# Five pieces of work in other places of a hand-ordered gated-mix backward kernel, steps 3 to 7

## The chip, the cores and the metric

The kernel runs on one core of a Trainium2 chip. A core has five engines, each with its own in-order instruction queue: TensorE (PE, matmuls; its weight loads are listed as PEld), VectorE (DVE), ScalarE (ACT), GpSimd (POOL) and SyncE (SP, which here only starts DMAs). They wait for each other on semaphores. SBUF is the working memory, PSUM takes the results of matmuls. The metric is the device time of one execution in microseconds (us).

## The reference

Forward, and then the gradients of all inputs but one, for 2048 tokens of width 576 in bf16:

```
g   = sigmoid((x * gate_w).sum(-1))                    # one gate a token
a   = irfft2(rfft2(x) * (w_r + 1j * w_i))              # spectral branch on A_x
b   = (gelu(x @ w_gate) * (x @ w_up)) @ w_down         # feed-forward branch, width 4608
out = g * a + (1 - g) * b
```

The outputs are `out` and the gradients with respect to x, w_r, w_i (2048 x 289), w_gate, w_up (576 x 4608), w_down (4608 x 576) and gate_w, given `grad_out` (dO). The feed-forward branch needs, for each feature, the gate and up products of x, the product z of dO with w_down, and from these the arrays A (gelu times up), dHg and dHu, which go into the weight gradients and, in the second stage, into `out` and the gradient of x.

## The kernel before

**Two stages.** Stage one takes the 4608 features in 18 groups of 256 (loop `g`, L992) and, within a group, the 16 token tiles of 128 in four steps of four tiles (loop `m`, L996). The step number is `pr = 4 g + m`, so steps 0 to 3 are group 0, steps 4 to 7 group 1. Stage two multiplies A, dHg and dHu, read back from DRAM, with the weights. The order of every engine's work is the order in which the Python code emits it: there is no scheduler.

**One step.** `H_mm` (L403) issues 16 + 4 matmuls for z (L413, L418) and the first four for gate|up (L422). `H_da` (L438) copies z out of PSUM on ACT, scaled by 1 - g (L441). Then `xy_full(0)` and `xy_full(1)` (L424) issue eight gate|up matmuls each (L429), a half each: two token tiles in one PSUM tile `xy`, of which there are two. With a second argument, `xy_full` calls that function between the two tiles of its half. `H_act` (L444) takes a half out of PSUM on ACT: part 1 copies gate to `xb` and up to `hu` (L450, L451), part 0 squares gate into `q` (L448). `H_ew1` (L453) computes the argument `s` of a sigmoid on DVE (L456 to L460).

**The held sigmoid.** `sigs` calls `H_ew2` (L471): a sigmoid on ACT (L476), eight DVE operations after it for groups 0 and 1 (L487 to L497), which give A, dHu and dHg, and a store of these that is put on a list and issued by SP at a later `flush`. In steps 0 to 3 `sigs` is put into `held` and called in the next step, between the halves of gate|up. From step 4 on it is called at the end of its own step, so that step 4 calls it twice: for step 3 and for itself.

**The rest of a step** is the weight gradient of the group before (`W_units`, L520), four matmuls at a time or eight: `u_dwd` for w_down (L541, with dO in `dB` as the streamed side), `u_dw` for gate|up (L559) and a tail (L573). Each unit has one of two PSUM tiles `wps` and ends with a copy `wevac` (L510) on ACT, or on DVE while `wcopy[0]` is `VC` (step 6). Step 4 issues the first 12 of 16 token tiles of two `u_dw` units, step 5 their last four and two `u_dwd`, step 6 the tail, two `u_dwd` and half a `u_dw`. Since `dB` must be scaled by 1 - g before `u_dwd` uses it, `scale_dB(k, ...)` (L985) scales token tiles 4k to 4k + 3, on ACT (L988) or DVE (L990).

**Spectral pieces** are small units (a list `fft`, L933) that `fft_next` emits one by one; `want` (L957) says how many a step has: one in step 6, four in step 7. In these steps they are by turns `u1` (L602: six matmuls, then an ACT copy Y, L607) and `u2` (L619: two matmuls, an ACT copy `ve`, L622, two DVE operations L624 and L625, a store). All use the one PSUM tile `z`, as does z of the steps. `k0` is 1 where the first piece of a step goes into `xy_full(1)`; before, that is so from step 8 on.

**Tables.** `build_R` (L157) makes integer angles on DVE in step 5; `build_B` (L215) is a generator, started in step 1 and resumed by `next(makeB)` twice in step 6: first nine DVE operations (L232 to L238), and at the end of the step one product (L248). Between them `run_late` (L114) emits five sines on ACT (L177, L245), with a table load before them and one before the next sigmoid.

Buffers that matter: `xb`, `hu` and `da` have two each; `q` and `s` one each from group 1 on, so that a new `q` waits until DVE has read the old one in L493.

Of the kernel before, what the change touches and what calls it, by code (L numbers as in the profile page):

```python
# [113 lines left out]
def run_late(tb):  # L114
    while tb.late:
        tb.late.pop(0)()
# [139 lines left out]
def kernel(  # L256
# [176 lines left out]
    def ewt(tag, g):  # L433
        if tag in ("q", "s", "sg"):
            return unit([4, FG], name=tag) if g == 0 else ew.tile([P, 4, FG], BF16, tag=tag, name=tag, bufs=1)
        return ew.tile([P, 4, FG], BF16, tag=tag, name=tag, bufs=2)

    def H_da(g, m, z):  # L438
        da = ewt("da", g)
        for t in range(4):  # L440
            nc.scalar.activation(da[:, t, :], z[:, t % 2, t // 2, :], ACT.Copy, scale=omg32[:, 4 * m + t:4 * m + t + 1])  # L441
        return da

    def H_act(k, xy, tiles, part):  # L444
        xb, q, hu = tiles
        h = slice(2 * k, 2 * k + 2)
        if part == 0:
            nc.scalar.activation(q[:, h, :], xy[:, :, 0:FG], ACT.Square)  # L448
        else:
            nc.scalar.copy(xb[:, h, :], xy[:, :, 0:FG])  # L450
            nc.scalar.copy(hu[:, h, :], xy[:, :, FG:2 * FG])  # L451
# [13 lines left out]
    def flush(n=9):  # L465

        while stores and n:
            stores.pop(0)()
            n -= 1
# [422 lines left out]
    VC, AC = V.tensor_copy, nc.scalar.copy  # L892
# [23 lines left out]
    makeB = build_B(nc, tb, unit, res)  # L916
# [20 lines left out]
    def fft_next():  # L937
        while fft_pos[0] < len(fft):
            u = fft[fft_pos[0]]
            fft_pos[0] += 1  # L940
            u()
            if not getattr(u, "noslot", False):
                return

    def ready():
        u = fft[fft_pos[0]]
        return not hasattr(u, "needs") or u.needs()
# [4 lines left out]
    NPR = NT // 2  # L952
# [4 lines left out]
    def want(pr):  # L957

        n0 = FIRST[-1]
        if pr < len(FIRST):  # L960
            return FIRST[pr]

        def load(n):

            return n + 0.5 * min(max(n - mid_at, 0), n_mid)
        share = load(n0) + (load(n_slots) - load(n0)) * (pr + 1 - len(FIRST)) / (LASTP - len(FIRST))
        n = n0
        while n < n_slots and load(n + 1) <= share + 1e-9:
            n += 1
        return int(min(n, n_slots) + 1e-9)  # L970
# [12 lines left out]
    carry, pend, held, rest = [], None, [], []  # L983

    def scale_dB(k, cp):  # L985
        for t in range(4 * k, 4 * k + 4):
            if cp == AC:
                nc.scalar.activation(dB[:, t, :], dB[:, t, :], ACT.Copy, scale=omg32[:, t:t + 1])  # L988
            else:
                V.tensor_scalar(dB[:, t, :], dB[:, t, :], omg32[:, t:t + 1], None, op0=ALU.mult)  # L990

    for g in range(NG):  # L992
        if g == 1:
            pgs.close()
            pw = ps1.enter_context(tc.tile_pool(name="pw", bufs=2, space=PSUM, **kw))
        for m in range(NPR):  # L996
            pr = g * NPR + m
            n = want(pr) - done[0]
            done[0] += n
            hs = [h for u in pend[m] for h in u] if pend else []  # L1000
            inside = pend[5].get(m, []) if pend else []

            def side_work(us):
                while side and us > 0:
                    us -= side[0][0]
                    side.pop(0)[1]()
            tiles = [ewt(tag, g) for tag in ("xb", "q", "hu")]
            state = []

            def sigs(g=g, m=m, tiles=tiles, state=state):  # L1010
                H_ew2(g, m, tiles, *state)
            if g == 0:
                def items(src, dst, t, *cp):
                    return titems(src, dst, 4 * t, (pgtile,) * 3, cp) if t < NPR else [None] * 3
                do1 = items(dB, dOT, 1, VC, VC, VC) if m == 0 else []
                do2 = items(dB, dOT, m + 2, AC, AC, VC)
                x1 = items(xn, xT, m + 1, AC if m else VC, VC, VC)
                z, xy_full = H_mm(g, m, ([opening] if m == 0 else []) + rest)
                rest = []
                da = H_da(g, m, z)  # L1020
                if m == 0:
                    early, mid_, late_ = do1[:2], [do1[2], x1[0]], x1[1:]
                elif m < NPR - 1:
                    early, mid_, late_ = x1[:1], x1[1:], []
                else:
                    early, mid_, late_ = [], [], []
                for f in early:
                    f()
                xy = xy_full(0)
                for f in mid_:  # L1030
                    f()
                if held:
                    held.pop()()
                for part in (1, 0):
                    H_act(0, xy, tiles, part)

                def between():
                    for f in late_:
                        f()
                xy = xy_full(1, between)  # L1040
                for part in range(2):
                    H_act(1, xy, tiles, part)
                if m == 0:
                    build_R(nc, tb, unit, 4)
                    columns_B(nc, tb, res)
                elif m == 1:
                    next(makeB)
                if m < NPR - 1:
                    gate(m + 1)
                else:  # L1050
                    V.tensor_copy(g32[:], g_bf[:])
                    V.tensor_scalar(gs32[:], g32[:], SD2, None, op0=ALU.mult)
                if m + 2 < NPR:
                    do2[0]()
                    rest = do2[1:]
                state += [*H_ew1(g, tiles, da), da]
                held.append(sigs)
            else:
                z, xy_full = H_mm(g, m)
                da = H_da(g, m, z)  # L1060
                for f in inside:
                    f()
                if pr == 5:
                    scale_dB(2, AC)
                xy = xy_full(0)
                if held:
                    scale_dB(0, AC)
                    held.pop()()
                for part in (1, 0):
                    H_act(0, xy, tiles, part)  # L1070
                k0 = int(n > 0 and pr > 7 and ready())
                xy = xy_full(1, fft_next if k0 else None)
                for part in range(2):
                    H_act(1, xy, tiles, part)
                if pr == 5:
                    scale_dB(3, VC)
                state += [*H_ew1(g, tiles, da), da]
                if pr == 4:
                    scale_dB(1, VC)
                elif pr == 5:  # L1080
                    build_R(nc, tb, unit, 8)
                    build_R(nc, tb, unit, 12)
                elif pr == 6:
                    next(makeB)
                side_work(4.4)
                jobs = carry + hs
                total = sum(w for w, _ in jobs)
                at, k = 0.0, k0
                tables = {6: 0}.get(pr)
                for i, (w, f) in enumerate(jobs):  # L1090
                    if k < n and (at >= total * k / n - 0.45 or len(jobs) - i <= n - k):
                        fft_next()
                        k += 1
                    if i == tables:
                        run_late(tb)
                        wcopy[0] = VC
                    if pr == NG * NPR - 1 and at == 0.0:
                        sigs()
                    f()
                    at += w  # L1100
                wcopy[0] = AC
                while k < n:
                    fft_next()
                    k += 1
                flush()
                if pr == 6:
                    next(makeB)
                if pr < NG * NPR - 1:
                    sigs()
            carry = []  # L1110
            if m < 3 and g + 1 < NG:
                load_w(g + 1, m)
            if done[0] == n_slots or (pr >= wgT_from and pr % 2 == 0 and len(wgT_all) < 20):
                load_wgT()
                if done[0] == n_slots:
                    load_wgT()
        carry = pend[4] if pend else []
        pend = W_units(g)
# [241 lines left out]
```

## Time and profile before

| | |
|---|---|
| runs, us | 1395.49, 1395.57, 1395.92, 1398.45 |
| median | 1395.75 |
| profiled execution | 1395.49, its span 1393.7 |
| PE / DVE / ACT busy over the span | 98% / 53% / 51% |
| step 3 (39.00 to 45.06 us) | 6.06 |
| step 4 (45.06 to 57.09) | 12.03 |
| step 5 (57.09 to 70.04) | 12.95 |
| step 6 (70.04 to 84.99) | 14.95 |
| step 7 (84.99 to 97.57) | 12.58 |
| step 8 (97.57 to 109.69) | 12.12 |

A step is cut here at the start of its first L413 matmul. In lists of groups or of the timeline a line gives the line of the code, the engine, the operation, the tiles (out<-in) and their shapes; `[0.61 <-ACT hu L451]` says that the engine stood for 0.61 us and that ACT's writing of `hu` in L451 ended it. In the list of waits the numbers are the total, the count and the longest. DVE and ACT are much fuller in steps 3 to 6 than over the whole span: 11.09 and 10.99 us of step 4's 12.03.

### The profile page before, as it was taken

What the parts mean: (1) busy time and instruction counts of PE and PEld (TensorE: products, weight loads), DVE (VectorE), ACT (ScalarE), POOL (GpSimd) and SP (SyncE); (2) the same over time, 40 slices, a digit from 0 to 9 for tenths busy, and PEclk for the clock granted to TensorE, in tenths of its full rate; (3) what the DMA queues carried; (4) which work ended last, traced back from release to release, by engine and by line L of the source; (5) the groups of instructions that cost most, each with busy time, mean ns of one, the idle gap of its engine ahead of it and who ended that gap; (6) DMA issues with size and microseconds to landing.
All of it is one profiled execution on the core that took longest, in us unless ns stands there. A gap on an engine that the chain in (4) does not pass through costs nothing.

```text
span 1393.7 us, 25930 instructions
## 1 busy us (share of the span) xinstructions
PE 1371.9 (98%) x10186; PEld 913.2 (66%) x10272; DVE 740.0 (53%) x1406; ACT 710.8 (51%) x1311; POOL 245.7 (18%) x486
## 2 busy tenths in 40 slices
PE   8999999999999999999999999999999999999999
PEld 6556566566556556556566566556777777777777
DVE  7975656555889777875656666560001742211101
ACT  7877767777787878767767777661000000000000
POOL 3001011123345634512111101110000100000000
PEclk9999999999999999999999999999999999999999
DMA  6433445355466556555556465749999998777773
GB/s 218 125 85 112 130 111 128 92 148 155 116 166 155 151 150 161 143 143 134 146 141 170 129 163 151 178 112 282 192 195 197 229 194 168 163 156 168 153 153 90
DMA packets 510647, 214.49 MB, mean 154 GB/s; under 512 B 312539, under 2 KB 503709, under 8 KB 510525
## 3 DMA queue, kind: packets, MB, share of 16 engines
q1 hardware_dynamic: 493402, 187.44, 57.2%
q0 software_dynamic: 14912, 24.24, 6.3%
q8 instruction: 80, 1.31, 0.4%
q10 hardware_dynamic: 2210, 1.15, 0.3%
q14 instruction: 43, 0.34, 0.1%
HBM read 41.05 MB, written 93.84 MB: 97 GB/s over the span
## 4 chain that ended last, share of the span: by engine, by line
PE 90%; ACT 2%; issue 1%; DMA 0%; SPq 0%; DVE 0%; ACTq 0%
PE acc L1210 30%; PE wps L559 16%; PE xy L429 15%; PE wps L541 9%; PE z L413 8%; PE wps L573 2%; PE xy L422 2%; PE pf L602 2%; PE z L418 1%; PE pf L619 1%; PE pf L873 1%; PE pf L800 1%; PE pf L711 1%; PE pf L875 1%; ACT ZT L850 0%
## 5 line engine op out<-in xcount | busy, mean ns | idle before, releaser
L1210 PEld LDWEIGHTS <-pin 128*128 128x128 bf16 x3456 | 338.0, 98 | 85.8 <-issue 0.3
L559 PE MATMUL wps<-dH,xn 128*128 128x512 bf16 x1135 | 269.9, 379 | 1.3 <-DVE dwd L510 0.5
L429 PE MATMUL xy<-wgu,xT 128*128 128x512 bf16 x1083 | 258.3, 379 | 8.3 <-issue 7.0
L429 PEld LDWEIGHTS <-xT 128*128 128x128 bf16 x1152 | 106.5, 98 | 133.0 <-issue 24.8
L559 PEld LDWEIGHTS <-xn 128*128 128x128 bf16 x1152 | 111.4, 98 | 118.7 <-issue 1.3
L1227 ACT COPY bo<-acc 128x288 f32<-128x288 f32 x32 | 12.8, 399 | 305.0 <-PE acc L1210 305.0
L541 PE MATMUL wps<-dB,A 128*128 128x288 bf16 x1152 | 154.2, 286 | 0.7 <-DVE dB L990 0.6
L566 POOL DMA_DIRECT2D out_dram<-dw x134 | 73.1, 549 | 432.4 <-ACT dw L510 390.4
L1210 PE MATMUL acc<-wgT,pin 128*128 128x288 bf16 x1152 | 143.8, 286 | 0.0
L1210 PE MATMUL acc<-wuT,pin 128*128 128x288 bf16 x1152 | 143.6, 286 | 0.0
L1210 PE MATMUL acc<-wd_all,pin 128*128 128x288 bf16 x1152 | 142.6, 286 | 0.0
L413 PE MATMUL z<-wdT,dOT 128*128 128x256 bf16 x1152 | 137.5, 273 | 1.2 <-ACT wdT L385 0.7
L541 PEld LDWEIGHTS <-A 128*128 128x128 bf16 x1152 | 112.1, 98 | 34.4 <-issue 1.3
L441 ACT ACTIVATE da<-z,omg 128x256 bf16<-128x256 f32 x288 | 112.3, 473 | 32.9 <-PE z L418 32.8
L413 PEld LDWEIGHTS <-dOT 128*128 128x128 bf16 x1152 | 112.4, 98 | 23.4 <-issue 2.4
L450 ACT CAST xb<-xy 128x512 bf16<-128x512 f32 x144 | 85.3, 593 | 48.1 <-PE xy L429 47.6
L1282 DVE SCALAR_TENSOR_TENSOR f32t<-gwf,dlog,b16t 128x576 f32<-128x576 f32 x16 | 13.1, 817 | 171.1 <-DMA b16t<-dxa_scr 171.1
L448 ACT ACTIVATE q<-xy 128x512 bf16<-128x512 f32 x144 | 87.9, 614 | 7.0 <-PE xy L429 4.7
L451 ACT CAST hu<-xy 128x512 bf16<-128x512 f32 x144 | 87.5, 608 | 0.0
L487 DVE TENSOR_TENSOR xb<-xb,sg 128x1024 bf16<-128x1024 bf16 x48 | 33.2, 691 | 96.6 <-ACT sg L479 96.5
L510 ACT CAST dw<-wps 128x512 bf16<-128x512 f32 x72 | 42.3, 590 | 54.5 <-PE wps L559 52.3
L456 DVE TENSOR_SCALAR s<-q 128x1024 bf16<-128x1024 bf16 x72 | 30.7, 426 | 69.8 <-ACT q L448 69.5
(220 smaller groups left out, 1634.1 us busy)
## 6 DMA issues: line engine op xcount, KB each, us to landing
scr<-dH SPq DMA_DIRECT2D x144, 256.0 KB, 3.4
scr<-A SPq DMA_DIRECT2D x72, 256.0 KB, 2.6
out_dram<-dw POOLq DMA_DIRECT2D x134, 64.0 KB, 2.5
wd_all<-in_B_w_down_dram SPq DMA_DIRECT2D x3, 1728.0 KB, 9.7
out_dram<-dwd POOLq DMA_DIRECT2D x34, 144.0 KB, 2.9
scr_p<-Vt SPq DMA_DIRECT2D x32, 145.0 KB, 2.8
wgu<-in_B_w_gate_dram SPq DMA_DIRECT2D x18, 256.0 KB, 4.2
wgu<-in_B_w_up_dram SPq DMA_DIRECT2D x18, 256.0 KB, 3.7
```

What stands on the lines that cost most here:

```text
L413: nc.tensor.matmul(zo(t), lhsT=dOT[:, ci, t, :], rhs=wdT[:, ci, :], start=(t % 4 < 2 and ci == 0), stop=False)
L429: nc.tensor.matmul(xy[k][:, t % 2, :], lhsT=xT[:, ci, t, :], rhs=wgu[:, ci, :], start=False, stop=(ci == 3))
L441: nc.scalar.activation(da[:, t, :], z[:, t % 2, t // 2, :], ACT.Copy, scale=omg32[:, 4 * m + t:4 * m + t + 1])
L448: nc.scalar.activation(q[:, h, :], xy[:, :, 0:FG], ACT.Square)
L450: nc.scalar.copy(xb[:, h, :], xy[:, :, 0:FG])
L451: nc.scalar.copy(hu[:, h, :], xy[:, :, FG:2 * FG])
L487: V.tensor_tensor(xb[:], xb[:], s[:], op=ALU.mult)
L510: wcopy[0](out, in_)
L541: nc.tensor.matmul(wps[:, :288], lhsT=tl(0, t)[:, fch * P:(fch + 1) * P], rhs=dB[:, t, h * 288:(h + 1) * 288], start=(t == 0), stop=(t == ...
L559: nc.tensor.matmul(wps[:].rearrange("p a b -> p (a b)"), lhsT=xn[:, t, c * P:(c + 1) * P], rhs=kt[t // 4][1][:, t % 4].rearrange("p k f -> ...
L566: wst[0].dma_start(ov[:, c, fsl], dw[:, k, :])
L1210: nc.tensor.matmul(acc[:, :288], lhsT=src[:, r, :], rhs=w_of(r)[:, h * 288:(h + 1) * 288], start=(first and r == 0), stop=(last and r == F ...
```

## The change

Five pieces of work take another place, and one of them another engine:

- In step 3 the held sigmoid (that of step 2) comes after the copies of the first gate|up half, not ahead of them. Steps 1, 2 and 4 stay.
- `scale_dB(2, ...)`, dO tiles 8 to 11, on ACT in both cases, moves from step 5 ahead of the gate|up halves to step 4 after the last copies.
- `scale_dB(3, ...)`, tiles 12 to 15, moves from DVE, after the copies of step 5, to ACT, ahead of them (where tiles 8 to 11 were).
- `next(makeB)`, the nine DVE operations of the table, moves in step 6 from after `H_ew1` to ahead of it.
- The condition for `k0` is `pr > 6`, so that in step 7 too the first spectral piece goes between the two tiles of the second gate|up half.

```diff
@@ -1029,10 +1029,12 @@
                 xy = xy_full(0)
                 for f in mid_:
                     f()
-                if held:
+                if held and m < NPR - 1:
                     held.pop()()
                 for part in (1, 0):
                     H_act(0, xy, tiles, part)
+                if held:
+                    held.pop()()
 
                 def between():
                     for f in late_:
@@ -1061,27 +1063,27 @@
                 for f in inside:
                     f()
                 if pr == 5:
-                    scale_dB(2, AC)
+                    scale_dB(3, AC)
                 xy = xy_full(0)
                 if held:
                     scale_dB(0, AC)
                     held.pop()()
                 for part in (1, 0):
                     H_act(0, xy, tiles, part)
-                k0 = int(n > 0 and pr > 7 and ready())
+                k0 = int(n > 0 and pr > 6 and ready())
                 xy = xy_full(1, fft_next if k0 else None)
                 for part in range(2):
                     H_act(1, xy, tiles, part)
-                if pr == 5:
-                    scale_dB(3, VC)
+                if pr == 4:
+                    scale_dB(2, AC)
+                elif pr == 6:
+                    next(makeB)
                 state += [*H_ew1(g, tiles, da), da]
                 if pr == 4:
                     scale_dB(1, VC)
                 elif pr == 5:
                     build_R(nc, tb, unit, 8)
                     build_R(nc, tb, unit, 12)
-                elif pr == 6:
-                    next(makeB)
                 side_work(4.4)
                 jobs = carry + hs
                 total = sum(w for w, _ in jobs)
```

## The prediction, made before the changed kernel ran

> **What bounds it now.** Five views, in this order. The page first: TensorE (PE) is busy 98% of the span, and the chain that ended last is 90% PE. So time can come only from the 2% in which PE stands.
>
> ```profile
> PE 1371.9 (98%) x10186; PEld 913.2 (66%) x10272; DVE 740.0 (53%) x1406; ACT 710.8 (51%) x1311; POOL 245.7 (18%) x486
> ```
>
> PE's waits over the whole span, each with the one that ended it, come second. The four that matter all lie between 45 and 98 us.
>
> ```profile
> PE pf L619 <- ACT Y L607: 0.7, 1, 0.7
> PE xy L422 <- ACT hu L451: 0.6, 1, 0.6
> PE wps L541 <- DVE dB L990: 0.6, 1, 0.6
> PE wps L559 <- DVE dwd L510: 0.5, 1, 0.5
> ```
>
> Idle time understates a stall here, because spans of pipelined matmuls overlap. So, third, I cut the span at the first z matmul (L413) of each step and set steps 4 to 8 beside a late step (68) that nothing holds up. The columns are the stretch, its length, then the busy times of PE, PEld, DVE, ACT and POOL, the granted clock (1.00 in all), the DMA share and GB/s.
>
> ```profile
> 45.06:57.09 12.03, 11.36 (x64) 5.80 (x64) 11.09 (x21) 10.99 (x22) 0.00 (x0) 1.00 0.30 89
> 57.09:70.04 12.95, 12.29 (x80) 7.26 (x80) 12.54 (x27) 9.36 (x18) 2.41 (x4) 1.00 0.63 179
> 70.04:84.99 14.95, 14.27 (x118) 9.51 (x118) 12.12 (x28) 11.65 (x21) 2.21 (x4) 1.00 0.45 103
> 84.99:97.57 12.58, 11.85 (x73) 6.45 (x72) 7.93 (x16) 9.73 (x18) 1.07 (x2) 1.00 0.11 36
> 97.57:109.69 12.12, 11.85 (x81) 7.23 (x81) 8.80 (x17) 8.58 (x16) 1.07 (x2) 1.00 0.33 101
> ...
> 891.16:902.64 11.48, 11.43 (x72) 6.50 (x72) 6.63 (x11) 7.79 (x14) 1.95 (x4) 1.00 0.64 147
> ```
>
> Step 68 holds 16 L559 and 16 L541 matmuls. By start-to-start time in the timeline an L559 costs 0.216 us, an L541 0.123, an L602 or L619 0.125; the L573 tail costs 1.87 (13.11 - 11.24, steps 70 and 67). Unheld, step 4 (24 L559) is step 67's 11.24; step 5 (8 L559, 32 L541) 11.48 - 1.73 + 1.96 = 11.71; step 6 (with tail and 6 L602) 14.33; step 7 11.5; step 8 11.75. The stalls are 0.79, 1.24, 0.62, 1.07 and 0.37: **4.1 us is all there is to win**, 0.3%.
>
> Fourth, the timeline at those places, one pair or triple for each stall.
>
> ```profile
> 44.11 1.06 ACT L476 ACTIVATE s<-s 128x1024 bf16<-128x1024 bf16 x1 [1.21 <-DVE s L457]
> ...
> 48.13 0.39 PE L422 MATMUL xy<-wgu,xT 64*128 64x512 bf16 x2 [0.61 <-ACT hu L451]
> ...
> 59.60 1.06 ACT L476 ACTIVATE s<-s 128x1024 bf16<-128x1024 bf16 x1 [3.54 <-DVE s L457]
> ...
> 66.71 1.20 DVE L990 TENSOR_SCALAR dB<-dB,omg 128x576 bf16<-128x576 bf16 x4
> 67.13 3.08 PE L541 MATMUL wps<-dB,A 128*128 128x288 bf16 x20 [0.61 <-DVE dB L990]
> ...
> 78.80 0.43 DVE L456 TENSOR_SCALAR s<-q 128x1024 bf16<-128x1024 bf16 x1 [1.40 <-ACT q L448]
> ...
> 82.77 0.81 DVE L510 CAST dwd<-wps 128x288 bf16<-128x288 f32 x2
> 83.27 1.89 PE L559 MATMUL wps<-dH,xn 128*128 128x512 bf16 x7 [0.47 <-DVE dwd L510]
> ...
> 90.86 1.08 ACT L448 ACTIVATE q<-xy 128x512 bf16<-128x512 f32 x2 [0.25 <-DVE xb L493]
> ...
> 93.51 0.41 PE L619 MATMUL pf<-Y,Rt 128*128 128x290 bf16 x2 [0.68 <-ACT Y L607]
> ```
>
> To see: the held sigmoid stops ScalarE (ACT) for 1.21 us while finished gate|up halves wait, and PE then waits for the last copy; ACT is empty for 3.54 us in step 4; PE waits for the third-last to last dO tiles (dB, t = 12 to 15) one by one; VectorE (DVE) is empty for 1.40 us in step 6 just ahead of table work that delays its two evacuations; PE waits for Y because its copy stands behind four others. Fifth, the waits of ACT and DVE gave the links below.
>
> **The change, part by part.** Nothing is added or removed: 8 scalings, one table build, one spectral piece, one sigmoid with its eight DVE operations change place or engine. None of the moved pieces issues a DMA of its own; the store of the sigmoid's products keeps its place in SP's queue and merely waits for a later DVE. ACT pitches (start to start): copy or square 0.48, sigmoid 0.96, da 0.357, dO scaling 0.666, Y 0.65.
>
> *Step 3, copies ahead of the sigmoid.* The first half of xy is done at 43.54 (a copy follows the eighth L429 by 0.42, as at 89.53). ACT then runs xb 43.54, hu 44.02, q 44.50, sigmoid 44.98, q 45.95, xb 46.44, hu 46.90 to 47.51, in place of 48.08. PE's L422 goes at 47.58, not 48.13: **-0.54**, with 0.25 of the stall left. The price: the sigmoid ends at 46.04, not 45.16, so DVE (11.09 busy of 12.03 us in step 4) starts L487 at 46.07 instead of 45.20. What is late next: s (L457) of step 3 at 52.75, the sigmoid behind it at 52.78 instead of 52.03, L487 at 53.87 instead of 53.17, so DVE stays 0.70 late; products of step 3 are ready at 59.13. PE, now 0.54 earlier, wants them for the last four token tiles of two dW units at 59.15 (59.69 before): cover of 1.26 us used up, stall 0.03 to 0.05.
>
> *Step 4, dO tiles 8 to 11 scaled in the empty stretch.* They run 56.59 to 59.42; the sigmoid that follows waits for s until 60.30 (59.60 + 0.70). Cost nothing: the 3.54 us cover them. Without that cover they would cost 4 x 0.666 = 2.7 us of ACT.
>
> *Step 5, tiles 12 to 15 scaled on ACT.* Here a rule speaks against the change: the Trainium skill, "ScalarE: Activation LUTs", section "Rules for kernel authors", sends a multiply to VectorE, up to about three times faster in bf16. The rows agree on the price: 0.280 a tile on DVE (L990), 0.666 on ACT (L988). By the rule the move is a loss: 4 x 0.39 = 1.5 us dearer, and ACT's copies behind it are late. By the rows DVE is late in its order, not slow: it reaches the four tiles at 66.71, behind eight products, and ACT reaches them after sigmoid 60.30, da 61.26 and two dw copies 62.69, from 63.63. They end at 64.45, 65.11, 65.78, 66.44. PE wants them at 65.86, 65.98, 66.10, 66.22, so only the last holds it, 0.27, where 1.24 was lost. I take the rows: PE's t = 15 goes at 66.49 instead of 67.96, **-1.47** in all. Queued behind on ACT: the copies of step 5, 0.69 later (q ends 68.38), so DVE's L456 starts at 68.41 instead of 67.83 although it lost 1.12 us of scaling. L422 of step 6 needs hu by 70.65 and has it at 69.35.
>
> *Step 6, table work ahead of the element-wise start.* DVE arrives 0.58 late (L497 ends 77.98). The nine operations L232 to L238 (1.68 us start to start, then 0.21) go from 77.90, L456 at 79.79 instead of 78.80, and the first dwd copy (L510) ends at 82.31 instead of 83.22: the 1.49 us gap in starts is filled, less the 0.58. PE would be at the next L559 at 81.17 and is let go at 82.36: a stall of 1.2, twice the old one. **PE's gain shrinks from 1.47 to 0.91.** On ACT, q of step 6 must wait until L493 of step 5 has read the old q (76.53): ACT is then 1.07 earlier, tables, sines and sigmoid included; the sines have their table input at 79.87 and want it at 83.
>
> *Step 7, the spectral piece between the halves.* PE's z starts at 84.08. Step 8 already has this order, so its offsets from z are the price: L602 +5.20, Y +6.14, q +7.00, hu +7.96, ve +8.44, next L602 +9.17 in place of +9.71. L619 no longer waits, but its copy ve now stands behind q, xb and hu, so the next L602 waits. L602 goes at 93.25 instead of 94.69: **-1.44**, and the rest of the step follows as before. No table load is added: L607 runs there today between sigmoids without one.
>
> Sum: 0.54 + 0.93 - 0.56 + 0.53 = 1.44. From step 8 on PE, ACT and the evacuations keep their order, the remaining waits are small, and PE leads, so the shift passes to the end. SP's weight loads for group 2, up to 0.7 later behind the late store, are issued by about 81 and first used at 97. The profiled execution took 1395.49 (span 1393.7 and 1.8 around it); less 1.44 that is 1394.05. The four runs have a median of 1395.75, 0.26 above it; I say **1394.1**.
>
> What the trace can't show: whether DVE's lateness of 0.88 is made good (0 to 0.9 at the dwd copy, I take 0.58, the chain above), whether ACT's last scaling meets PE (0 to 0.5, I take 0.27), and where the table work's buffers, wanted 3 us earlier, are free (below zero excluded; their last users seem done, I take 0). Together these make gains of 0.6 to 2.5.
>
> **Rivals.** A, the forecast: stalls move and shrink, 1393.1 to 1395.0. B, every stall named goes and no new one comes: DVE takes no harm from the later sigmoid and the dwd copy is ready in time. Then 2.8 to 4.1 us, most likely 3.3: 1392.3. For it: each edit sits at one of the four waits. Against: DVE is 92 to 97% busy in steps 4 and 5, so work pushed back there stays back. C, PE's gain is eaten by a later release that doesn't move, a load or the chain through the one z buffer: about 1395.6. Against: no DMA among PE's waits after step 0. D, slower: DVE's lateness grows at each sigmoid handshake (steps 3, 4, 5), as each waits for s and s for the copies. The place is L510 in step 6: the filled gap gives 1.49, so beyond 1.49 us late PE leaves later than 83.27, one for one. With 0.88 lost at each of three handshakes, 2.6, it is 1.1 worse: 1396.7; twice as much per handshake makes 1399. Against: the trace gives ACT 0.4 to 0.9 us of slack at two of them.
>
> **How the numbers follow.** A measurement of this kernel can tell about 0.2%, 2.8 us, from no change. A has 0.54, B 0.27, C 0.09, D 0.10. B lies beyond 2.8 but for its lower edge (0.25 faster); D's upper part gives 0.07 slower; the rest, 0.68, is within. The range reaches into B's middle and D's lower part: 1391.9 to 1396.4.
>
> **What would show it.** Right: L422's wait at 47.6 falls to under 0.3; the waits for dB go; L559 waits for dwd longer than 0.5; the wait of L619 turns into one of L602 for ve; step 5 lasts about 12.0, step 7 about 12.0. Wrong: a wait on dH (L559) near 59, a wait on dB left at 1 us, or the dwd wait gone, which is B. The shift of the first z of step 8, 97.57 now, should equal the change of the span.

## The result and the profile after

The changed kernel takes 1394.38 us in the median (1394.05 to 1395.89), the kernel before, measured beside it, 1395.63 (1395.49 to 1398.45). The ratio is 0.9990, with a 95% interval of 0.9986 to 0.9994: faster by 0.1%. The interval leaves out 1, but the step is smaller than the 0.2% that the prediction took as the least a measurement can tell from no change. Eight of the changed kernel's 41 executions, with a mean clock of 0.999 and not 1.000, took 1395.7 to 1395.9, the others 1394.05 to 1394.71; the last section shows two executions of that kind. The profiled execution took 1394.12, and its span fell from 1393.7 to 1392.3 us, by 1.4.

The steps of the changed kernel, cut again at the first z matmul of steps 4 to 8 (stretch, length, then PE, PEld, DVE, ACT, POOL busy, granted clock, DMA share, GB/s):

```profile
45.12:56.57 11.45, 11.36 (x64) 5.80 (x64) 9.89 (x18) 10.37 (x20) 0.00 (x0) 1.00 0.24 70
56.57:68.64 12.07, 11.88 (x81) 7.33 (x80) 10.73 (x21) 11.19 (x21) 2.41 (x4) 1.00 0.66 187
68.64:84.17 15.53, 14.27 (x118) 9.51 (x118) 14.03 (x32) 12.70 (x24) 2.21 (x4) 1.00 0.46 120
84.17:96.17 12.00, 11.72 (x72) 6.46 (x72) 7.90 (x15) 9.48 (x18) 1.07 (x2) 1.00 0.11 37
96.17:108.30 12.13, 11.85 (x81) 7.24 (x81) 8.81 (x17) 8.58 (x16) 1.07 (x2) 1.00 0.33 102
```

Step 4 is 0.58 us shorter than before (its ends are rounded), step 5 0.88 and step 7 0.58 shorter; step 6 is 0.58 *longer*. The waits of PE from 38 to 105 us, which is from step 3 into step 8 (total, count, longest), tell the same:

```profile
PE wps L559 <- DVE dwd L510: 1.0, 1, 1.0
PE xy L429 <- issue: 0.3, 2, 0.2
PE pf L602 <- ACT ve L622: 0.2, 1, 0.2
```

Of the four waits shown before, three are gone from the list (hu, dB, Y). The fourth, for dwd in step 6, has doubled from 0.5 to 1.0, and a small one for ve, in step 7, is new. The timeline of the changed kernel at those places, with the same columns as before:

```profile
45.04 1.07 ACT L476 ACTIVATE s<-s 128x1024 bf16<-128x1024 bf16 x1
...
46.14 0.69 DVE L487 TENSOR_TENSOR xb<-xb,s 128x1024 bf16<-128x1024 bf16 x1 [1.08 <-ACT s L476]
...
47.19 0.81 PE L422 MATMUL xy<-wgu,xT 64*128 64x512 bf16 x4
...
56.67 2.81 ACT L988 ACTIVATE dB<-dB,omg 128x576 bf16<-128x576 bf16 x4
...
60.37 1.06 ACT L476 ACTIVATE s<-s 128x1024 bf16<-128x1024 bf16 x1 [0.88 <-DVE s L457]
...
63.70 2.80 ACT L988 ACTIVATE dB<-dB,omg 128x576 bf16<-128x576 bf16 x4
64.44 4.37 PE L541 MATMUL wps<-dB,A 128*128 128x288 bf16 x32
...
68.49 0.43 DVE L456 TENSOR_SCALAR s<-q 128x1024 bf16<-128x1024 bf16 x1 [0.93 <-ACT q L448]
...
76.71 1.08 ACT L448 ACTIVATE q<-xy 128x512 bf16<-128x512 f32 x2 [0.60 <-DVE xb L493]
...
79.88 0.42 DVE L456 TENSOR_SCALAR s<-q 128x1024 bf16<-128x1024 bf16 x1
81.94 0.81 DVE L510 CAST dwd<-wps 128x288 bf16<-128x288 f32 x2
82.45 1.89 PE L559 MATMUL wps<-dH,xn 128*128 128x512 bf16 x7 [1.05 <-DVE dwd L510]
...
93.34 0.91 PE L602 MATMUL pf<-Dt,xT 128*128 128x290 bf16 x6 [0.22 <-ACT ve L622]
```

To see: in step 3 ACT no longer waits ahead of the sigmoid, but DVE now waits 1.08 us for it, in a stretch where it has little room. In step 5 PE runs through its 32 L541 matmuls in 4.37 us (4.08 in step 6, where nothing holds them, so 0.29 is left). DVE has a new gap of 0.93 us at 68.49, waiting for q behind the four scalings on ACT, and none ahead of L456 in step 6.

### The profile page after: what moved, and what is told of

It is laid out like the page before. It is cut to its first block, busy times and chain, and to the rows that moved or that the text cites. A ratio compares the mean times of both kernels' runs of the same rounds, so it can differ in the third digit from the quotient of the medians.

```text
span 1392.3 us, 25932 instructions
## 1 busy us (share of the span) xinstructions
PE 1371.3 (98%) x10186; PEld 913.3 (66%) x10272; DVE 738.9 (53%) x1402; ACT 713.4 (51%) x1315; POOL 245.9 (18%) x486
## 4 chain that ended last, share of the span: by engine, by line
PE 93%; ACT 3%; DVE 3%; issue 1%; ACTq 0%; DMA 0%; SPq 0%; DVEq 0%
PE acc L1212 30%; PE wps L559 16%; PE xy L429 16%; PE wps L541 9%; PE z L413 8%; PE wps L573 2%; PE xy L422 2%; PE pf L602 2%; PE z L418 2%; PE pf L873 1%; PE pf L619 1%; PE pf L800 1%; PE pf L711 1%; PE pf L875 1%; ACT ZT L850 0%
## 5 line engine op out<-in xcount | busy, mean ns | idle before, releaser
L559 PE MATMUL wps<-dH,xn 128*128 128x512 bf16 x1136 | 270.1, 379 | 1.9 <-DVE dwd L510 1.0
L559 PEld LDWEIGHTS <-xn 128*128 128x128 bf16 x1152 | 111.5, 98 | 119.4 <-issue 1.9
L541 PE MATMUL wps<-dB,A 128*128 128x288 bf16 x1152 | 153.7, 286 | 0.2
L541 PEld LDWEIGHTS <-A 128*128 128x128 bf16 x1152 | 112.2, 98 | 33.4 <-issue 0.3
L456 DVE TENSOR_SCALAR s<-q 128x1024 bf16<-128x1024 bf16 x72 | 30.6, 426 | 70.0 <-ACT q L448 69.9
```

Source lines behind the costliest of these rows:

```text
L541: nc.tensor.matmul(wps[:, :288], lhsT=tl(0, t)[:, fch * P:(fch + 1) * P], rhs=dB[:, t, h * 288:(h + 1) * 288], start=(t == 0), stop=(t == ...
L559: nc.tensor.matmul(wps[:].rearrange("p a b -> p (a b)"), lhsT=xn[:, t, c * P:(c + 1) * P], rhs=kt[t // 4][1][:, t % 4].rearrange("p k f -> ...
```

## The experiments

The quantity that tells kernels apart best is the start of each step's first z matmul. Step 0 differs by up to 1.7 us between executions before it reaches anything that was changed, so each shift below is against the kernel before and less the kernel's own shift by the start of step 3. From step 8 to step 71 no shift moves by more than 0.05 us. In us, with a minus for earlier:

| kernel | step 5 | step 6 | step 7 | step 8 |
|---|---|---|---|---|
| changed | -0.57 | -1.46 | -0.88 | -1.45 |
| sigmoid ahead of the copies again | 0.00 | -1.24 | -1.60 | -1.92 |
| sigmoid after xb alone | -0.49 | -1.73 | -1.76 | -2.34 |
| dO scaled as before (both runs) | -0.57 | +0.71 | +0.09 | +0.03 |
| table work after again | -0.57 | -1.46 | -0.89 | -1.42 |
| piece after the halves | -0.57 | -1.47 | -0.89 | -1.03 |
| last four scalings left out | -0.57 | -1.76 | -1.81 | -2.39 |
| sigmoid after xb, one tile earlier | -0.49 | -1.73 | -2.32 | -2.41 |
| table move alone | 0.00 | 0.00 | -0.63 | -0.04 |

The theory to be tested is the one that the forecast's sum rests on: ACT and DVE hand work back and forth, and what a part wins for PE at its own place can be taken back later by the lateness it leaves on one of them. The rival is that the parts add up.

**The sigmoid ahead of the copies again.** Step 3's order is that of the kernel before, the rest is the changed kernel:

```diff
-                if held and m < NPR - 1:
+                if held:
                     held.pop()()
                 for part in (1, 0):
                     H_act(0, xy, tiles, part)
-                if held:
-                    held.pop()()
```

> The changed kernel with its first part undone: in step 3 the held sigmoid is again ahead of the copies. My theory: that part's 0.54 us at step 4 is paid back in step 6, because the sigmoid that ends 0.88 later keeps VectorE late up to the two dwd copies that PE waits for. Without it PE's L422 stands 0.6 us again in step 4, but VectorE is in time: L510 ends near 81.6 instead of 82.4, PE's L559 after it goes at 81.7, and the first z of step 8 comes 1.8 us earlier than in the kernel before (1.39 in the changed one). Span 1391.9. Rival, the parts add up: the 0.54 is lost and nothing comes back; first z of step 8 only 0.85 earlier, span 1392.85.

Measured: 1393.91 us, ratio to the kernel before 0.9985 (0.9976 to 0.9994), span 1391.8, first z of step 8 1.92 earlier. Its timeline:

```profile
44.11 1.06 ACT L476 ACTIVATE s<-s 128x1024 bf16<-128x1024 bf16 x1 [1.21 <-DVE s L457]
...
48.13 0.39 PE L422 MATMUL xy<-wgu,xT 64*128 64x512 bf16 x2 [0.61 <-ACT hu L451]
...
79.10 0.42 DVE L456 TENSOR_SCALAR s<-q 128x1024 bf16<-128x1024 bf16 x1
81.17 0.89 DVE L510 CAST dwd<-wps 128x288 bf16<-128x288 f32 x2
81.67 1.89 PE L559 MATMUL wps<-dH,xn 128*128 128x512 bf16 x7
```

The stall in step 4 is back as it was, and yet PE starts step 7 0.72 us earlier than in the changed kernel, because DVE's L456 and dwd copies are earlier by as much (0.78 in the two timelines, before their offsets are taken off). So **the first part of the change cost 0.47 us net**: its lead of 0.57 at step 5 is 0.22 at step 6, a lag of 0.72 at step 7, and 0.47 of that stays. The parts don't add up.

**The sigmoid after xb alone.**

```diff
-                if held and m < NPR - 1:
+                if m < NPR - 1:
+                    if held:
+                        held.pop()()
+                    for part in (1, 0):
+                        H_act(0, xy, tiles, part)
+                else:
+                    nc.scalar.copy(tiles[0][:, 0:2, :], xy[:, :, 0:FG])
                     held.pop()()
-                for part in (1, 0):
-                    H_act(0, xy, tiles, part)
-                if held:
-                    held.pop()()
+                    nc.scalar.copy(tiles[2][:, 0:2, :], xy[:, :, FG:2 * FG])
+                    H_act(0, xy, tiles, 0)
```

The two `nc.scalar.copy` are those of part 1 of `H_act`, for xb (now L1038) and hu.

> The changed kernel, but in step 3 only the copy of gate (xb) goes ahead of the held sigmoid; up and the square follow it. The copy fits into the 1.2 us in which ScalarE waits for s, so the sigmoid runs at 44.1 as in the kernel before. My theory: PE gets 0.47 us at step 4 and VectorE isn't late, so both gains stand: L422 goes at 47.65, PE loses nothing to dO in step 5, L559 goes at about 81.55 in step 6, first z of step 8 2.1 us earlier than before, span 1391.6. Rival, order of these copies doesn't matter and VectorE's lateness is of no account: as the changed kernel, 1.39 earlier, span 1392.3.

Measured: 1393.22 us, ratio 0.9980 (0.9972 to 0.9989), span 1391.4, first z of step 8 2.34 earlier. Its timeline:

```profile
43.59 0.58 ACT L1038 CAST xb<-xy 128x512 bf16<-128x512 f32 x1 [0.64 <-PE xy L429]
44.16 1.06 ACT L476 ACTIVATE s<-s 128x1024 bf16<-128x1024 bf16 x1
45.25 0.69 DVE L487 TENSOR_TENSOR xb<-xb,s 128x1024 bf16<-128x1024 bf16 x1 [0.19 <-ACT s L476]
47.19 0.89 PE L422 MATMUL xy<-wgu,xT 64*128 64x512 bf16 x4
...
81.56 1.89 PE L559 MATMUL wps<-dH,xn 128*128 128x512 bf16 x7 [0.43 <-DVE dwd L510]
```

One copy fits into ACT's wait for s, so the sigmoid isn't late, DVE waits 0.19 us and not 1.08, and PE still wins 0.49 in step 4. It beats both kernels: against the kernel before by median and interval, against the changed one (0.9986 to 0.9994) by the shift, 0.9 us, while the intervals of the ratios still overlap.

**dO scaled as before**, both moves of `scale_dB` undone, the rest changed:

```diff
-                    scale_dB(3, AC)
+                    scale_dB(2, AC)
...
-                if pr == 4:
-                    scale_dB(2, AC)
+                if pr == 5:
+                    scale_dB(3, VC)
```

> The changed kernel with both moves of the dO scaling undone (tiles 8 to 11 on ScalarE in step 5, 12 to 15 on VectorE after the copies of step 5). My theory: VectorE, 0.7 us late through the later sigmoid, reaches the four tiles 0.7 later, so PE's t = 15 goes at about 68.6 (67.96 before, 66.56 changed), the stall grows to about 2.4 us, and nearly all of the change's gain goes: first z of step 8 within 0.2 us of the kernel before, span 1393.5 to 1394.0. Rival, the parts add up: only the part's own 0.9 us goes, first z 0.5 earlier than before, span 1393.2.

> The kernel with both moves of the dO scaling undone, once more, since its first run lost 1.7 us in step 0, ahead of anything that was changed. My theory as before: first z of step 8 within 0.2 us of the kernel before, span 1393.5 to 1394.0. Rival as before: first z 0.5 earlier, span 1393.2.

The first run has a span of 1395.4 and one time of 1397.31, of which 1.7 us were lost in step 0. The second: 1396.29 us, ratio 1.0005 (0.9994 to 1.0017), span 1394.2. From step 3 to step 8 both runs agree to 0.01 us: step 6 starts 0.71 later than in the kernel before, step 8 0.03 later. All of the change's gain is gone with these two moves; no run undid one of them alone. PE's waits in step 5 of the second run:

```profile
66.96 0.28 PE L541 MATMUL wps<-dB,A 128*128 128x288 bf16 x1 [0.38 <-ACT dB L988]
68.29 3.08 PE L541 MATMUL wps<-dB,A 128*128 128x288 bf16 x20 [1.05 <-DVE dB L990]
```

One wait was not foreseen: tile 11, scaled on ACT in the late order, is late too.

**Table work after again**, the rest changed:

```diff
                 if pr == 4:
                     scale_dB(2, AC)
-                elif pr == 6:
-                    next(makeB)
...
                     build_R(nc, tb, unit, 12)
+                elif pr == 6:
+                    next(makeB)
```

> The changed kernel with the table work back behind the element-wise start of step 6. My theory: the gap that it was to fill is no longer there, since VectorE comes 0.6 us late and the square of step 6 is there when it comes; the two dwd copies end at the same time (82.4, within 0.15), first z of step 8 as in the changed kernel within 0.1 us, span 1392.2 to 1392.5. Rival, the move fills the 1.4 us gap of the kernel before: without it the dwd copies and PE are 0.6 us or more later in step 6, span 1392.9 or more.

Measured: 1394.05 us (one time), span 1392.3, first z of step 8 1.42 earlier, within 0.03 of the changed kernel. Its timeline:

```profile
77.93 0.42 DVE L456 TENSOR_SCALAR s<-q 128x1024 bf16<-128x1024 bf16 x1
...
81.89 0.81 DVE L510 CAST dwd<-wps 128x288 bf16<-128x288 f32 x2
82.39 1.89 PE L559 MATMUL wps<-dH,xn 128*128 128x512 bf16 x7 [1.04 <-DVE dwd L510]
```

L456 starts without a wait, so there is no gap for the table work to fill, and PE's wait for dwd is there with 1.04 us. In the changed kernel the table's place is worth nothing.

**The table move alone**, in the kernel before:

```diff
                     scale_dB(3, VC)
+                elif pr == 6:
+                    next(makeB)
...
-                elif pr == 6:
-                    next(makeB)
```

> The kernel before with the table work moved up in step 6 and nothing else. Here VectorE's gap of 1.4 us is there to be filled. My theory: L510 ends near 81.9, PE's wait for dwd goes, and the first z of step 7 is 0.6 us earlier than in the kernel before; but ScalarE's row from step 6 (which the move doesn't touch) sets Y and ve of step 7, so that the first z of step 8 is within 0.1 us of the kernel before, span 1393.6 to 1393.8. Rival, PE keeps what it wins: first z of step 8 0.6 earlier, span 1393.1.

Measured: one time of 1397.07 and a span of 1395.3, with 1.6 us lost in step 0; first z of step 7 0.63 earlier, of step 8 0.04. Here the gap is there and PE does win its 0.63 in step 6. It then waits for Y in step 7:

```profile
PE pf L619 <- ACT Y L607: 1.3, 1, 1.3
```

That wait was 0.7 in the kernel before: the gain is given back whole, one step later, to ACT.

**The piece after the halves**, the rest changed (`pr > 7` for `pr > 6`):

> The changed kernel with the spectral piece of step 7 back behind both halves. My theory: the piece saves only the part of L619's wait that ve's later place on ScalarE doesn't take: the next L602 would go 0.4 us later than in the changed kernel, first z of step 8 about 1.0 earlier than in the kernel before (1.39 in the changed one), span 1392.7. Rival: the whole stall of step 7 in the kernel before (1.07 us, 0.57 of it gone in the changed kernel) comes back, first z of step 8 at most 0.8 earlier, span 1392.9.

Measured: 1394.5 us (one time), span 1392.7, first z of step 8 1.03 earlier: the part is worth 0.42 us. PE's waits from 38 to 105 us:

```profile
PE wps L559 <- DVE dwd L510: 1.0, 1, 1.0
PE pf L619 <- ACT Y L607: 0.6, 1, 0.6
```

**The last four scalings left out**, so that their part of the gradient of w_down stays unscaled.

```diff
-                if pr == 5:
-                    scale_dB(3, AC)
```

> The changed kernel without the scaling of dO tiles 12 to 15 at all (that part of the gradient of w_down is left unscaled, so the time is that of a kernel with less work). It prices these four instructions where the change has put them. My theory: they aren't free on ScalarE. They hold back the copies of step 5 by 2.7 us, of which 1.0 reaches VectorE's L456 (the new q must wait for L493 anyway) and from there the dwd copies; L510 ends near 81.4, first z of step 8 about 2.3 us earlier than in the kernel before (1.39 in the changed one), span 1391.4. Rival: ScalarE has room and the only price is the rest of PE's own wait for the last tile, 0.3 us, which step 6 takes away again: first z 1.4 to 1.7 earlier, span 1392.0 to 1392.3.

Measured: 1393.3 us (one time), span 1391.4, first z of step 8 2.39 earlier. The wait for dwd shrinks from 1.05 to 0.41 us. Here is what moves DVE: q starts at 66.23 instead of 67.32, held now by DVE's own L493, and L456 at 67.51 instead of 68.49.

```profile
66.23 1.08 ACT L448 ACTIVATE q<-xy 128x512 bf16<-128x512 f32 x2 [1.39 <-DVE xb L493]
...
67.51 0.42 DVE L456 TENSOR_SCALAR s<-q 128x1024 bf16<-128x1024 bf16 x1
...
81.56 1.89 PE L559 MATMUL wps<-dH,xn 128*128 128x512 bf16 x8 [0.41 <-DVE dwd L510]
```

So four scalings in the place that the change gives them cost 0.94 us of the end; at step 6, where PE's own wait for dO is all that tells the two apart, it was 0.3.

**The sigmoid after xb alone, and tile 12 scaled in step 4.** The third argument of `scale_dB` is new: the number of tiles to leave out at the start.

```diff
                 if pr == 5:
-                    scale_dB(3, AC)
+                    scale_dB(3, AC, 1)
...
                 if pr == 4:
                     scale_dB(2, AC)
+                    nc.scalar.activation(dB[:, 12, :], dB[:, 12, :], ACT.Copy, scale=omg32[:, 12:13])
```

> The kernel with the sigmoid after xb alone, and dO tile 12 scaled in step 4 too, in what is left of ScalarE's empty stretch there. My theory: ScalarE's copies of step 5 end 0.67 earlier, VectorE's L456 and the dwd copies with them, and PE's wait for dwd in step 6 (0.4 idle) goes, so the first z of step 7 is 0.5 earlier than with the sigmoid after xb alone. But from step 6 ScalarE's row of copies, five sines and two table loads is what step 7 waits for, and that starts with PE's first half of step 6, which doesn't move: first z of step 8 2.3 to 2.5 us earlier than in the kernel before, span 1391.2 to 1391.4. Rival, step 7 follows PE: first z of step 8 2.8 earlier, span 1390.9.

Measured: 1393.40 us, ratio 0.9984 (0.9975 to 0.9993), span 1391.7, first z of step 7 2.32 earlier, of step 8 2.41. The wait for dwd is gone and step 7 starts 0.56 earlier than without this edit, but step 8 only 0.07 earlier, and the times show no gain over it. Of PE's waits from 38 to 105 us only that for ve is left, 0.7 us of it in step 7, and the timeline says where it comes from:

```profile
PE pf L602 <- ACT ve L622: 0.9, 2, 0.7
```

```profile
83.25 1.28 ACT L476 ACT_TABLE_LOAD   x1
...
85.63 0.69 DVE L487 TENSOR_TENSOR xb<-xb,s 128x1024 bf16<-128x1024 bf16 x1 [1.94 <-ACT s L476]
...
88.75 0.69 DVE L493 TENSOR_TENSOR xb<-xb,q 128x1024 bf16<-128x1024 bf16 x1
...
89.53 0.60 ACT L448 ACTIVATE q<-xy 128x512 bf16<-128x512 f32 x1 [0.85 <-DVE xb L493]
```

ACT waits 0.85 us with q of step 7 until DVE has read the old q, and DVE got there late because its sigmoid stood behind the sines and two table loads. The first of the two table loads starts, after each kernel's own offset, at the same time as without this edit (78.98 and 78.63). So that row on ACT looks like the next bound; no run moved it.

## Why the prediction was right

It said 1394.1, measured 1394.38; a fall of 1.44 in the profiled span, measured 1.38 (1.45 from the start of step 3 to step 8). Its range, 1391.9 to 1396.4, also holds the kernel before, so the time alone says little for it. What does is that PE's shift was followed from step to step and came out within 0.03 us at each. Two of its parts were nevertheless valued wrongly, the sigmoid's and the table's.

*Step 3, copies ahead.* Forecast -0.54, measured -0.57, with 0.2 of PE's stall left (0.25 forecast). The sigmoid ended at 46.11 (46.04), and DVE was late as worked out; the products for the two dW units were there for PE's L559 at 59.26 without a listed wait. The forecast treated this part as a gain that is later shared. By the first experiment it is a loss of 0.47. The chain of starts in the prediction held that answer, but it was followed for the whole change only and not with one part taken out.

*Step 4, tiles 8 to 11 at no cost.* They ran from 56.67 to 59.49, and the sigmoid after them waited 0.88 us more for s. Right.

*Step 5, tiles 12 to 15 on ACT.* PE waited for the last four tiles, t = 12 to 15, as the numbers in the prediction say (its "third-last to last" is three). Forecast -1.47 in all, measured -1.46, and q and L456 late as stated (68.41, measured 68.49). The Trainium skill's rule ("ScalarE: Activation LUTs", section "Rules for kernel authors": multiply on VectorE) and the rows were weighed, and the rows won: with both moves undone and these tiles on DVE in their old place the whole gain is lost. No run put them on DVE in an earlier place, so what the engine and what the place is worth is not told apart. But the rule's objection is real in this place as well: the experiment without these scalings shows 0.94 us, where the prediction's sum named 0.27 of PE's own wait and 0.58 of DVE's lateness.

*Step 6.* The shrinking of PE's gain to 0.91 was measured as 0.88, the idle time before L559 as 1.05 (a stall of 1.2 forecast). What failed in this step is the value given to the table move: "the 1.49 us gap in starts is filled, less the 0.58". The arithmetic of the starts holds, but the gap closed by itself, since PE and ACT came 1.4 and 1.0 us earlier and with them the q that L456 waits for. With the table work in its old place the dwd copies end within 0.05 us of the same time (after each kernel's own offset). So the sum came out right with a part in it that does nothing. Alone, in the kernel before, it does win, and then step 7 takes the gain away.

*Step 7.* L602 was forecast at 93.25 and went at 93.34, 0.06 of that from step 0; the piece was to be worth 0.4 in its experiment and was worth 0.42. The wait changed from Y to ve, as named.

Neither rival B (the dwd wait would have gone), C (a shift lost later: none is, up to step 71) nor D (the first dwd copy ending later than 83.22: it ends at 82.39) came about.

## What to carry to other kernels

Where two engines hand work to each other in turn, value a move by following the starts to the next place where the bound engine waits for either of them; a gain at the edited line is worth nothing until it has passed there. Put into an engine's wait only as much as the wait holds: one copy ahead of the sigmoid won for PE nearly what three won (0.49 and 0.57 us) and left the other engine on time. And take parts out one at a time even when the sum comes out right: here one of five parts cost 0.47 us, one was worth nothing, and the gain went when the two moves of dO were undone.

## What the runs showed of the hardware

Two of the profiled executions, one of them the first with dO scaled as before, lost 1.6 to 1.7 us in step 0, ahead of every edit. The granted clock shows how. That run in stretches of 2 us, columns as above:

```profile
12.00:14.00 2.00, 1.99 (x36) 1.42 (x36) 1.62 (x10) 1.90 (x5) 0.00 (x0) 1.00 0.99 389
14.00:16.00 2.00, 1.03 (x10) 0.95 (x9) 1.95 (x7) 1.89 (x6) 0.00 (x0) 0.73 1.01 396
16.00:18.00 2.00, 1.78 (x5) 0.66 (x5) 1.31 (x3) 0.99 (x3) 0.00 (x0) 0.50 1.03 389
18.00:20.00 2.00, 2.00 (x19) 1.23 (x18) 0.78 (x2) 1.02 (x3) 0.00 (x0) 0.92 1.08 253
```

A mean of 0.73 over 2 us is 1.1 us at half clock, 0.50 is 2.0 and 0.92 is 0.3: the clock is halved from about 14.9 us for some 3.4 us, and step 1 then starts 1.6 us late. In the other such run, that of the table move alone, it is halved for as long, from about 14.8. The kernel before was granted 1.00 over the same stretch, though PE was as sparsely busy there (2.05 of 3 us from 14 to 17).

The length agrees with the Trainium skill ("TensorE: Matmul & The Clock Gate", part 1), which has the clock set by a free-running window of about 3.4 us, and to half after an idle window. But PE was not idle for so long here: from 11.50 to 14.91 us it was busy for 2.14 of 3.41 us, with 0.96 us as its longest wait, and in the kernel before for 2.06. Why one execution loses the clock and another doesn't stays open; no run moved the thin stretch. The practical side is shown: the loss is as large as the whole effect of this change, so a single time of such a kernel says little below 2 us, and the shift of a landmark against an earlier landmark in the trace says a lot.
